# Moving the next head's product, the W3 and W4 reads and the output buffers in a fused attention, MLP and gradient kernel

## The chip, the core and the metric

The kernel runs on one core of a Trainium2 chip. The metric is the time of one execution on the device in microseconds (us), the median over repeated runs. All tensors are bfloat16 in DRAM; sums are kept in float32.

The engines of the core work side by side, each through its own list of instructions in order: PE multiplies matrices, DVE does elementwise work and reductions, ACT scales, copies and takes exponentials, POOL and SP here only issue DMAs. A DMA is issued on an engine's queue (SP's or POOL's here) and carried out by 16 DMA engines that all queues share.

## What is computed

One query token of width 640 passes through an attention over 32 heads, each with its own cache of 8192 keys and 8192 values of width 192, and then an MLP; the results are the output and the gradients of a scalar product with `grad_out` in nine inputs.

```python
# forward
mod = silu(c) @ w_mod                       # six vectors: sa, ca, ga, sb, cb, gb
h   = layernorm(x) * (1 + ca) + sa
q   = h @ wq                                # 32 heads of 192
p   = softmax(q K^T / sqrt(192))            # per head, over 8192 keys
o   = p V
x   = x + ga * (o @ wo)
h   = layernorm(x) * (1 + cb) + sb
x   = x + gb * (h + gelu(layernorm(h) @ w3) @ w4)   # the mixer part falls away in what is differentiated and shown here
...
# backward: out_0 = x; out_1.. = gradients of A_x, k_cache, v_cache, wq, wo, w3, w4, c, w_mod
```

Nearly all bytes are in the caches: K and V are 100.7 MB each, and so are their gradients dK and dV. V is read twice, once in the forward part and once in the backward part; dK and dV are outer products (a column of weights over the keys times a row of 192) and are only written.

## The kernel before

**Tiles.** A head's K or V is cut into two halves, each one tile of 128 partitions by 32 keys by 192 (1536 KB, called t = 0 and 1). Scaling and multiplying go by quarters of a head (q = 0 to 3, 16 keys per partition).

**Forward part.** The loop at L545 runs over i = 1 to 33 and has three heads in flight. For head i it makes the scores and the softmax; for head i-1 it scales K by the exponentials; for head i-2 and i-1 it multiplies V by scaled K on PE. Its pieces, by name:

- `fwd_load` (L331) reads a half of V of head i-1 and the same half of K of head i+1, both through SP. V tiles come from the pool `fv` with three buffers, K tiles from `big` with five (and every sixth from a pool of one).
- `fwd_mult(h, t)` (L344) multiplies a half of K by q on DVE, into a tile `prod` of a pool with two buffers. `fwd_ssum(h, t)` (L352) adds its 24 pieces up on PE; `fwd_red` (L361) and `fwd_comb` (L365) finish the scores, `fwd_max` (L373) spreads the maximum, and `fwd_exp` (L376) takes the negative maximum on DVE (`negm`), the exponential on ACT (`E_f`), and copies of it on DVE (`P2h`, `E_all`).
- `fwd_scale(h, q)` (L405) scales a quarter of K into a tile EK: 8 of its 16 rows on ACT (L391), the rest on DVE (L399). It needs `E_f` and `P2h`.
- `fwd_kv(h, q)` (L434) is the multiplication of V by EK, in three parts A, B and K; its last reader sets V's and EK's buffers free. `fwd_keep` and `fwd_keepB` (L453, L464) take a head's result out of PSUM.

In an iteration the order was: scale(i-1, 0 and 1), ssum(i, 0), mult(i, 1), kv(i-2, 2 and 3), scale(i-1, 2), mult(i+1, 0), keep and keepB of head i-2, ssum(i, 1), red(i), scale(i-1, 3), kv(i-1, 0), the maximum, kv(i-1, 1), exp(i).

**Between the parts.** W3 (640 by 1536) and W4 (1536 by 640) lie in tiles `w_t` of `big`. They were read by four DMAs of POOL (L557 to L562): W3 and seven of twelve row blocks of W4 in iteration 31, the last five in iteration 32. `dg_some` (L504) makes 12 dot products with W4 on DVE. From the last head's result a chain of small steps leads over two layernorms, `u` (L736, W3), the transposed W3 (L631), `dn2` (L764) and wo to `do`, and then to the first dV tile (L1079).

**Backward part.** The loop at L1083 runs over i = 0 to 31, from the last head down. Per head: `bwd_dv` (L898) makes two dV tiles, 20 of 32 rows on ACT and the rest on DVE; `bwd_mult` (L889) multiplies both halves of V by do on DVE and adds up on PE; `bwd_ds` (L911); `bwd_dk` (L918) makes two dK tiles on DVE. dV and dK tiles come from the five buffers of `big` and are written by POOL's DMAs (L909, L924). Other gradients (wo, w3, w4, wq, w_mod) are spread over the iterations as jobs J0, J1 and J2; the jobs for wq and w_mod have pools of their own (`side`), whose last use is in iteration 24.

**Order.** `pin_order` (L53) fixes the order of PE, DVE and ACT to that of the text of the kernel. The order on SP and POOL, and which free buffer a tile gets, is settled when the program is built.

Of the kernel before, what the change touches and what calls it, by code (L numbers as in the profile page):

```python
# [9 lines left out]
BF16 = mybir.dt.bfloat16  # L10
# [10 lines left out]
def kernel(  # L21
# [26 lines left out]
    nc = tc.nc  # L48
# [16 lines left out]
    P = 128  # L65
    D = A_x.shape[-1]
    _, HQ, S, DH = A_k_cache.shape
# [156 lines left out]
    def big_tile(name):  # L224
        return big.tile([P, JH, DH], BF16, name=name, tag="big")
# [105 lines left out]
    def fwd_load(h, t):  # L331
        if 0 <= h < HQ:
            st[h]["V"].append(load_v(fv, h, t))
        if h + 2 < HQ and (h + 2, t) not in K_st:
            K_st[h + 2, t] = load_k(h + 2, t)
# [37 lines left out]
    def fwd_max(h, st):  # L373
        nc.tensor.matmul(st["sm"][:, P : 2 * P], lhsT=st["m1"].to_broadcast([P, P]), rhs=ident_f, start=True, stop=True)

    def fwd_exp(h, st):  # L376
        negm = fsm.tile([P, 1], FP32, name="negm")
        nc.vector.tensor_reduce(out=negm, in_=st["sm"][:, P : 2 * P], axis=AX.X, op=ALU.max, negate=True)  # L378
        E_f = fsm.tile([P, J], FP32, name="E_f")
        nc.scalar.activation(out=E_f, in_=st["sm"][:, 0:J], func=ACT.Exp, bias=negm, scale=1.0, accum_out=rowsum[:, h : h + 1])  # L380
        P2h = fsm.tile([P, J, 2], BF16, name="P2h")
        nc.vector.tensor_copy(out=P2h, in_=E_f[:, :, None].to_broadcast([P, J, 2]))
        nc.vector.tensor_copy(out=E_all[:, h, :], in_=E_f)
        st["E_f"], st["P2h"], st["EK"] = E_f, P2h, []
# [20 lines left out]
    def fwd_scale(h, q, st):  # L405
        fwd_scale_act(h, q, st)
        fwd_scale_dve(h, q, st)
# [26 lines left out]
    def fwd_kv(h, q, st):  # L434
        fwd_kvA(h, q, st)
        fwd_kvB(h, q, st)
        fwd_kvK(h, q, st)

    def fwd_wo(h, st):
        if h % 2 == 1:  # L440
            c0 = 3 * (h // 2)
            st["wo"] = fwo.tile([P, 3, D], BF16, name="wo_t")
            nc.sync.dma_start(out=st["wo"], in_=wo_v[:, c0 : c0 + 3, :])
# [51 lines left out]
    def flat(tl):  # L495
        return tl.rearrange("p j d -> p (j d)")

    def w3n(i, lo, hi):
        return w_t[0][:, i * F + lo : i * F + hi] if i < 4 else w_t[1][:, lo:hi]

    def w4n(f, lo, hi):
        return w_t[1][:, F + f * D + lo : F + f * D + hi] if f < 7 else w_t[2][:, (f - 7) * D + lo : (f - 7) * D + hi]

    def dg_some(f0, f1):  # L504
        jk_t = fpr.tile([P, JH, DH], BF16, name="prod").rearrange("p j d -> p (j d)")
# [39 lines left out]
    for i in range(1, HQ + 2):  # L545
        if i == HQ + 1:
            nc.scalar.activation(out=warm, in_=eps_c, func=ACT.Sqrt)
        c, p, pp = 2 <= i < HQ, 0 <= i - 1 < HQ, 0 <= i - 2 < HQ
        n = i + 1 < HQ
        fwd_load(i - 1, 0)  # L550
        if p:
            fwd_scale(i - 1, 0, st[i - 1])
            fwd_scale(i - 1, 1, st[i - 1])
        fwd_load(i - 1, 1)
        if i == HQ - 1:
            w_t = [flat(big_tile(f"w_t{k}")) for k in range(2)]
            nc.gpsimd.dma_start(out=w_t[0].rearrange("p (i n) -> p i n", n=F), in_=B_w3[0 : 4 * P, :].rearrange("(i p) n -> p i n", p=P))  # L557
            nc.gpsimd.dma_start(out=w_t[1][:, 0:F], in_=B_w3[4 * P : 5 * P, :])
            nc.gpsimd.dma_start(out=w_t[1][:, F : F + 7 * D].rearrange("p (f n) -> p f n", n=D), in_=B_w4[0 : 7 * P, :].rearrange("(f p) n -> p f n", p=P))
        if i == HQ:  # L560
            w_t.append(flat(big_tile("w_t2")))
            nc.gpsimd.dma_start(out=w_t[2][:, 0 : 5 * D].rearrange("p (f n) -> p f n", n=D), in_=B_w4[7 * P : 12 * P, :].rearrange("(f p) n -> p f n", p=P))  # L562
        if p:
            fwd_wo(i - 1, st[i - 1])
        if c:
            fwd_ssum(i, 0, st[i])
            fwd_mult(i, 1, st[i])
        if i % 2 == 1 and n:
            q_pb[(i + 1) // 2] = pair_bc(fsm, q_bf, (i + 1) // 2, "q_pb", st[max(i - 1, 1)]["sm"])
        if i % 2 == 0 and i >= 4:  # L570
            fwd_ao((i - 4) // 2, st[i - 3]["wo"], st[i - 1]["sm"])
            fwd_ao_add((i - 4) // 2, st[i - 1]["sm"])
        if pp:
            fwd_kv(i - 2, 2, st[i - 2])
            fwd_kvA(i - 2, 3, st[i - 2])
            fwd_kvB(i - 2, 3, st[i - 2])
            fwd_kvK(i - 2, 3, st[i - 2])
        if i > HQ:
            dg_some(7, NFC)
        if p:  # L580
            fwd_scale(i - 1, 2, st[i - 1])
            if i % 2 == 0:
                fwd_tot(i - 1, st[i - 1]["sm"])
        if n:
            fwd_mult(i + 1, 0, st[i + 1])
        if pp:
            fwd_keep(i - 2, st[i - 2])
            fwd_keepB(i - 2, st[i - 2])
            if i % 2 == 1:
                fwd_o((i - 2) // 2)  # L590
        if p and i % 2 == 0:
            fwd_rinv(i - 1, st[i - 1]["sm"])
        if c:
            fwd_ssum(i, 1, st[i])
            fwd_red(i, st[i])
        if p:
            fwd_scale(i - 1, 3, st[i - 1])
            if i == 1:
                q_out(1, NWQ)
            fwd_kvA(i - 1, 0, st[i - 1])  # L600
            fwd_kvB(i - 1, 0, st[i - 1])
        if c:
            fwd_comb(i, st[i])
        if p:
            fwd_kvK(i - 1, 0, st[i - 1])
        if c:
            fwd_max(i, st[i])
        if p:
            fwd_kv(i - 1, 1, st[i - 1])
        if c:  # L610
            fwd_exp(i, st[i])
        if i == HQ:
            dg_some(0, 7)
    SB = [1024]
    w_t.append(flat(big_tile("w_t3")))
    NB3 = JH * DH // P
# [1 line left out]
    def w3T(blk, n=1):  # L618
        if blk < NB3:
            return w_t[3][:, blk * P : (blk + n) * P]  # L620
        c0 = 5 * D + (blk - NB3) * P
        return w_t[2][:, c0 : c0 + n * P]

    w3T_next = [0]
# [264 lines left out]
    def bwd_mult(h, t):  # L889
# [5 lines left out]
            nc.tensor.matmul(bst[h]["dP_ps"][:, t * JH : (t + 1) * JH, :], lhsT=ident_bf, rhs=V_sb[:, :, k * DS : (k + 1) * DS], start=(k == 0), stop=(k == NDS - 1))  # L895
        freed.add(("v", h, t))

    def bwd_dv(h, t, na=NAV // 2, parts=1):  # L898
        o = big_tile("dV")
        j0 = t * JH  # L900
        doh = vec_of(do_pb, h)
        for jj in range(na):
            nc.scalar.activation(out=o[:, jj, :], in_=doh, func=ACT.Copy, scale=bst[h]["PF"][:, j0 + jj : j0 + jj + 1])  # L903
        n = JH // parts
        for r0 in range(0, JH, n):
            r1 = r0 + n
            ra = max(r0, na)
            pairs_outer(o[:, ra:r1, :], bst[h]["P2h"][:, j0 + ra : j0 + r1, :], doh, r1 - ra)
            st2.dma_start(out=dV_hd[h][:, j0 + r0 : j0 + r1, :], in_=o[:, r0:r1, :])  # L909
# [6 lines left out]
        bst[h]["dS2"] = dS2  # L916

    def bwd_dk(h, t, parts=1):  # L918
        o = big_tile("dK")
        n = JH // parts  # L920
        for r0 in range(0, JH, n):
            j0 = t * JH + r0
            pairs_outer(o[:, r0 : r0 + n, :], bst[h]["dS2"][:, j0 : j0 + n, :], vec_of(q_pb, h), n)
            st2.dma_start(out=dK_hd[h][:, j0 : j0 + n, :], in_=o[:, r0 : r0 + n, :])  # L924
# [93 lines left out]
    NPH = 10  # L1018
# [64 lines left out]
    for i in range(HQ):  # L1083
        h, nxt = HS[i], HS[i + 1] if i + 1 < HQ else None
        if i % 2 == 1 and nxt is not None:
            bwd_dob(nxt // 2)
        for f in J0[i]:
            f()
        if i <= AHEAD:
            for t in range(2):  # L1090
                bwd_mult(h, t)
        ring_load()
        if i - 1 in dq:
            fin_dq(*dq.pop(i - 1))
        if i == 0:
            fin_c_copy(PS[0], 1, c_first)
        if nxt is not None:
            bwd_pf(nxt)
            for t in range(2):
                bwd_dv(nxt, t)  # L1100
        if i < NPH:
            hook(i)
        if i == 3:
            bcast_cols(du_bf, 0, NFC, du_bc, act_copy)
        for f in J1[i]:
            f()
        bwd_ds(h)
        if i >= AHEAD and nxt is not None:
            for t in range(2):
                bwd_mult(nxt, t)  # L1110
        bwd_dk(h, 0)
        bwd_dk(h, 1, 1 if nxt is not None else 4)
        if i in cps:
            fin_c_copy(*cps.pop(i))
        if i == 1:
            mid_cols()
            job_mid()
            dve_copy(dmod_bf[:, 2 * NDC : 6 * NDC], dmod_c[:, 2 * NDC : 6 * NDC])
        if i == NPH - 1:
            fin_dq(*dq.pop(i))  # L1120
            for cm in reversed(mm_cms):
                cm.__exit__(None, None, None)
            for nm, b in (("in", 1), ("out", 4), ("bc", 1)):
                side[nm] = ctx.enter_context(tc.tile_pool(name="side" + nm, bufs=b, side="right", reuse_waits="tile"))
        for f in J2[i]:
            f()
    pin_order(first_ins)


# [28 lines left out]
```

## Time and profile before

| | |
|---|---|
| time, median of 3 runs | 1394.95 us (1394.62 to 1397.5) |
| the profiled execution's own time | 1396.62 us |
| its span, first to last instruction | 1394.8 us |
| DMA | 570.81 MB, 409 GB/s over the span |
| of it through SP's queue | 339.16 MB |
| of it through POOL's queue | 229.85 MB |
| DVE busy | 1078.9 us (77%) |
| ACT busy | 964.2 us (69%) |
| PE busy | 856.1 us (61%) |

A row of the stretches view gives, for a stretch of the span, each engine's busy time with its count of instructions, the clock that PE was granted as a share of full speed, the share of time that the 16 DMA engines were busy, and the bytes that they moved per second. A row of the timeline gives start, length, engine, line, operation and tiles, and in brackets how long the engine stood idle just before and what ended that. The forward part runs to about 560 us, the steps between the parts to about 581 us, the backward part to the end. Iteration 24 of the backward loop ends at 1246 us.

### The profile page before, as it was taken

The page shows a single profiled execution, that of the slowest core. Times are in us where ns is not written, and L with a number is a line of the kernel's source. Part 1 is how long each engine was busy: PE and PEld are TensorE (multiplying, and loading weights), DVE is VectorE, ACT ScalarE, POOL GpSimd, SP SyncE. Part 2 cuts the span into 40 slices and gives each one's busy share as a digit, 9 for nine tenths or more (in the row PEclk, how much of TensorE's full clock was granted, in tenths as well). Part 3 has the DMA queues.
Part 4 walks back from the last instruction along what each step waited for, and adds up shares of the span by engine and source line. Part 5 has one row for each costly group of instructions (what it writes and reads, how often), then busy time and mean ns, then how long its engine had stood idle before and what let it go on. Part 6 is the DMA issues. An engine that isn't in the chain of part 4 may idle for free. (4 is left out here: it accounts for less than half of the span.)

```text
span 1394.8 us, 28118 instructions
## 1 busy us (share of the span) xinstructions
PE 856.1 (61%) x11519; PEld 672.9 (48%) x11519; DVE 1078.9 (77%) x1276; ACT 964.2 (69%) x2633; POOL 114.9 (8%) x207
## 2 busy tenths in 40 slices
PE   3699999999999999737635642443432435323342
PEld 3577777777777777626525541322222223212231
DVE  3588878878888886699988984975768659666796
ACT  1487778877777787786795586566766766566582
POOL 0000000000000000011101110211111111111011
PEclk9799999999999999666656665666675666755666
DMA  9999999999999999699999999999999999999988
GB/s 392 418 420 417 415 410 416 418 404 402 418 412 408 413 417 403 241 384 397 426 427 425 425 428 427 427 427 427 427 427 424 424 424 419 426 409 416 407 352 367
DMA packets 71711, 570.81 MB, mean 409 GB/s; under 512 B 6878, under 2 KB 18398, under 8 KB 31134
## 3 DMA queue, kind: packets, MB, share of 16 engines
q1 hardware_dynamic: 46496, 339.16, 59.2%
q0 software_dynamic: 25056, 229.85, 39.1%
q8 instruction: 90, 1.47, 0.4%
q14 instruction: 39, 0.32, 0.1%
q10 hardware_dynamic: 30, 0.00, 0.0%
HBM read 343.08 MB, written 225.91 MB: 408 GB/s over the span
## 5 line engine op out<-in xcount | busy, mean ns | idle before, releaser
L903 ACT ACTIVATE dV<-do_pb,PF 128x192 bf16<-128x192 bf16 x1260 | 439.3, 440 | 90.9 <-DMA out_dram<-dK 60.6
L895 PE MATMUL dP_ps<-V_sb,ident_bf 128*128 128x256 bf16 x1536 | 232.1, 326 | 258.6 <-DVE V_sb L131 258.6
L391 ACT ACTIVATE EK<-K_sb,E_f 128x192 bf16<-128x192 bf16 x1024 | 364.5, 442 | 22.1 <-PE kb_ps L432 14.0
L895 PEld LDWEIGHTS <-ident_bf 128*128 128x128 bf16 x1536 | 179.4, 117 | 311.0 <-issue 177.9
L880 DVE TENSOR_TENSOR dK<-dS,q_pb 128x6144 bf16<-128x6144 bf16 (+1 forms) x67 | 213.2, 3211 | 47.0 <-DMA out_dram<-dK 43.2
L131 DVE TENSOR_TENSOR prod<-K_sb,q_pb 128x6144 bf16<-128x6144 bf16 x64 | 214.6, 3354 | 23.5 <-DMA K_sb<-in_A_k_cache_dram 18.0
L131 DVE TENSOR_TENSOR V_sb<-V_sb,do_pb 128x6144 bf16<-128x6144 bf16 x64 | 211.8, 3350 | 6.6 <-DMA V_sb<-in_A_v_cache_dram 6.6
L416 PE MATMUL ps_a<-EK,V_sb 128*128 128x193 bf16 x2048 | 202.1, 252 | 3.1 <-DMA V_sb<-in_A_v_cache_dram 2.3
L416 PEld LDWEIGHTS <-V_sb 128*128 128x128 bf16 x2048 | 175.6, 100 | 21.8 <-issue 17.4
L880 DVE TENSOR_TENSOR dV<-P2h,do_pb 128x2304 bf16<-128x2304 bf16 (+1 forms) x65 | 87.2, 1368 | 56.1 <-DMA out_dram<-dV 44.0
L399 DVE TENSOR_TENSOR EK<-K_sb,P2h 128x1536 bf16<-128x1536 bf16 x128 | 121.6, 950 | 0.0
L424 PE MATMUL ps_b<-EK,V_sb 128*64 128x193 bf16 x2048 | 110.8, 250 | 8.2 <-DVE MB_all L134 7.9
L359 PE MATMUL S_ps<-prod,ident_bf 64*64 64x256 bf16 x3072 | 99.7, 277 | 7.2 <-DVE prod L131 7.2
L424 PEld LDWEIGHTS <-V_sb 128*64 128x64 bf16 x2048 | 84.4, 109 | 28.9 <-issue 28.7
L359 PEld LDWEIGHTS <-ident_bf 64*64 64x64 bf16 x3072 | 82.3, 109 | 22.8 <-issue 22.3
L380 ACT ACTIVATE E_f<-sm_ps,negm 128x64 f32<-128x64 f32 x32 | 10.1, 315 | 104.9 <-DVE negm L378 104.9
L909 POOL DMA_DIRECT2D out_dram<-dV x65 | 34.8, 535 | 462.6 <-ACT dV L903 313.7
L432 PE MATMUL kb_ps<-EK,hot_bf 128*32 128x384 bf16 x1024 | 65.9, 335 | 2.0 <-DVE q_bf L304 2.0
L981 PEld LDWEIGHTS <-ident_bf 128*128 128x128 bf16 x112 | 14.5, 130 | 91.4 <-issue 88.9
L194 ACT CAST do_pb<-bc_ps 128x384 bf16<-128x384 f32 x16 | 7.5, 470 | 69.0 <-PE bc_ps L190 69.0
L939 ACT ACTIVATE wq_o<-wq_bc,ha_f 128x1536 bf16<-128x1536 bf16 x12 | 18.5, 1565 | 47.8 <-DMA out_dram<-wq_o 47.8
L924 POOL DMA_DIRECT2D out_dram<-dK x67 | 37.1, 554 | 165.0 <-DVE dK L880 126.5
(249 smaller groups left out, 821.8 us busy)
## 6 DMA issues: line engine op xcount, KB each, us to landing
V_sb<-in_A_v_cache_dram SPq DMA_DIRECT2D x126, 1536.0 KB, 11.8
K_sb<-in_A_k_cache_dram SPq DMA_DIRECT2D x64, 1536.0 KB, 13.7
out_dram<-dV POOLq DMA_DIRECT2D x63, 1536.0 KB, 18.5
out_dram<-dK POOLq DMA_DIRECT2D x63, 1536.0 KB, 20.8
wq<-in_A_wq_dram SPq DMA_DIRECT2D x3, 2560.0 KB, 33.9
wo_t<-in_A_wo_dram SPq DMA_DIRECT2D x16, 480.0 KB, 12.4
out_dram<-dwo POOLq DMA_DIRECT2D x16, 480.0 KB, 19.5
wq<-in_A_wq_dram SPq DMA_DIRECT2D x4, 1920.0 KB, 29.7
```

Source lines behind the costliest of these rows:

```text
L131: nc.vector.tensor_tensor(out=out, in0=a, in1=b, op=ALU.mult)
L359: nc.tensor.matmul(st["S_ps"][c0 : c0 + 64, r, t * JH : (t + 1) * JH, :], lhsT=ident_bf[64 * r : 64 * r + 64, 64 * r : 64 * r + 64], rhs=p ...
L391: nc.scalar.activation(out=EK[:, jj, 0:DH], in_=K_st[h, t][:, r * JQ + jj, :], func=ACT.Copy, scale=st["E_f"][:, j : j + 1])
L399: nc.vector.tensor_tensor(out=EK[:, NA:JQ, 0:DH].rearrange("p j (d r) -> p j d r", r=2), in0=K_st[h, t][:, r * JQ + NA : (r + 1) * JQ, :]. ...
L416: nc.tensor.matmul(st["A_ps"][:, 0 : DH + 1], lhsT=V_sb[:, r * JQ + jj, a0:a1], rhs=EK[:, jj, 0 : DH + 1], start=(q == 0 and jj == 0), sto ...
L424: nc.tensor.matmul(st["B_ps"][g : g + 64, 0 : DH + 1], lhsT=V_sb[:, r * JQ + jj, b0:b1], rhs=EK[:, jj, 0 : DH + 1], start=(q == 0 and jj < ...
L432: nc.tensor.matmul(kb_ps[g : g + 32, 0 : 2 * DH], lhsT=hot_bf[:, HQ - 1 - h : 2 * HQ - 1 - h], rhs=EK[:, jj : jj + 2, 0:DH], start=(h == 0 ...
L880: nc.vector.tensor_tensor(out=o.rearrange("p j (d r) -> p j d r", r=2), in0=pairs[:, :, None, :].to_broadcast([P, n, NP2, 2]), in1=vec.rea ...
L895: nc.tensor.matmul(bst[h]["dP_ps"][:, t * JH : (t + 1) * JH, :], lhsT=ident_bf, rhs=V_sb[:, :, k * DS : (k + 1) * DS], start=(k == 0), sto ...
L903: nc.scalar.activation(out=o[:, jj, :], in_=doh, func=ACT.Copy, scale=bst[h]["PF"][:, j0 + jj : j0 + jj + 1])
L909: st2.dma_start(out=dV_hd[h][:, j0 + r0 : j0 + r1, :], in_=o[:, r0:r1, :])
L924: st2.dma_start(out=dK_hd[h][:, j0 : j0 + n, :], in_=o[:, r0 : r0 + n, :])
```

## The change

Four things are moved or added.

- `fwd_mult(i+1, 0)` is no longer done behind scale(i-1, 2), but inside `fwd_exp(i)`: on DVE between `negm` and `P2h`.
- `fwd_kv(i-2, 2)` stands ahead of `fwd_ssum(i, 0)` on PE instead of behind it.
- W3 and W4 are read by SP instead of POOL, cut otherwise: nine row blocks of W4 into the first tile in iteration 31 (ahead of the second half of V of head 30), then in iteration 32, behind V of the last head, three blocks of W4 and two of W3 into the second tile and three of W3 into the third. `dg_some` is cut 9 and 3 instead of 7 and 5.
- Behind the jobs of iteration 24 the `side` pools are closed and a pool `more` with three tiles is opened. From iteration 25 the tiles for dV and dK come from eight buffers: of each eight tiles the first, fourth and sixth from `more`, the others from `big`.

```diff
-    def fwd_exp(h, st):
+    def fwd_exp(h, st, between=lambda: None):
         negm = fsm.tile([P, 1], FP32, name="negm")
         nc.vector.tensor_reduce(out=negm, in_=st["sm"][:, P : 2 * P], axis=AX.X, op=ALU.max, negate=True)
         E_f = fsm.tile([P, J], FP32, name="E_f")
         nc.scalar.activation(out=E_f, in_=st["sm"][:, 0:J], func=ACT.Exp, bias=negm, scale=1.0, accum_out=rowsum[:, h : h + 1])
+        between()
         P2h = fsm.tile([P, J, 2], BF16, name="P2h")
...
+    w_t = []
+    W4_N, W3_N = 9, 2
+    W4_R = NFC - W4_N
+
     def w3n(i, lo, hi):
-        return w_t[0][:, i * F + lo : i * F + hi] if i < 4 else w_t[1][:, lo:hi]
+        c0 = W4_R * D + i * F if i < W3_N else (i - W3_N) * F
+        return w_t[1 if i < W3_N else 2][:, c0 + lo : c0 + hi]
 
     def w4n(f, lo, hi):
-        return w_t[1][:, F + f * D + lo : F + f * D + hi] if f < 7 else w_t[2][:, (f - 7) * D + lo : (f - 7) * D + hi]
+        c0 = f % W4_N * D
+        return w_t[f // W4_N][:, c0 + lo : c0 + hi]
+
+    def load_wt(k):
+        w_t.append(flat(big_tile(f"w_t{k}")))
+        if k < 2:
+            f0, f1 = (0, W4_N) if k == 0 else (W4_N, NFC)
+            nc.sync.dma_start(out=w_t[k][:, 0 : (f1 - f0) * D].rearrange("p (f n) -> p f n", n=D), in_=B_w4[f0 * P : f1 * P, :].rearrange("(f p) n -> p f n", p=P))
+        if k > 0:
+            i0, i1, c0 = (0, W3_N, W4_R * D) if k == 1 else (W3_N, NDC, 0)
+            nc.sync.dma_start(out=w_t[k][:, c0 : c0 + (i1 - i0) * F].rearrange("p (i n) -> p i n", n=F), in_=B_w3[i0 * P : i1 * P, :].rearrange("(i p) n -> p i n", p=P))
...
+        if i == HQ - 1:
+            load_wt(0)
         fwd_load(i - 1, 1)
-        if i == HQ - 1:
-            w_t = [flat(big_tile(f"w_t{k}")) for k in range(2)]
-            nc.gpsimd.dma_start(out=w_t[0].rearrange("p (i n) -> p i n", n=F), in_=B_w3[0 : 4 * P, :].rearrange("(i p) n -> p i n", p=P))
-            nc.gpsimd.dma_start(out=w_t[1][:, 0:F], in_=B_w3[4 * P : 5 * P, :])
-            nc.gpsimd.dma_start(out=w_t[1][:, F : F + 7 * D].rearrange("p (f n) -> p f n", n=D), in_=B_w4[0 : 7 * P, :].rearrange("(f p) n -> p f n", p=P))
-        if i == HQ:
-            w_t.append(flat(big_tile("w_t2")))
-            nc.gpsimd.dma_start(out=w_t[2][:, 0 : 5 * D].rearrange("p (f n) -> p f n", n=D), in_=B_w4[7 * P : 12 * P, :].rearrange("(f p) n -> p f n", p=P))
         if p:
             fwd_wo(i - 1, st[i - 1])
+        if i == HQ:
+            load_wt(1)
+            load_wt(2)
+        if pp:
+            fwd_kv(i - 2, 2, st[i - 2])
         if c:
             fwd_ssum(i, 0, st[i])
             fwd_mult(i, 1, st[i])
...
         if pp:
-            fwd_kv(i - 2, 2, st[i - 2])
             fwd_kvA(i - 2, 3, st[i - 2])
...
         if i > HQ:
-            dg_some(7, NFC)
+            dg_some(9, NFC)
...
-        if n:
-            fwd_mult(i + 1, 0, st[i + 1])
...
+        first = lambda: fwd_mult(i + 1, 0, st[i + 1]) if n else None
         if c:
-            fwd_exp(i, st[i])
+            fwd_exp(i, st[i], first)
+        else:
+            first()
         if i == HQ:
-            dg_some(0, 7)
+            dg_some(0, 9)
...
+    more, out_n = [None], [0]
+
+    def out_tile(name):
+        if more[0] is None:
+            return big_tile(name)
+        out_n[0] += 1
+        if out_n[0] % 8 in (1, 4, 6):
+            return more[0].tile([P, JH, DH], BF16, name=name, tag="more")
+        return big_tile(name)
+
     def bwd_dv(h, t, na=NAV // 2, parts=1):
-        o = big_tile("dV")
+        o = out_tile("dV")
...
     def bwd_dk(h, t, parts=1):
-        o = big_tile("dK")
+        o = out_tile("dK")
...
-            for nm, b in (("in", 1), ("out", 4), ("bc", 1)):
-                side[nm] = ctx.enter_context(tc.tile_pool(name="side" + nm, bufs=b, side="right", reuse_waits="tile"))
+            side_cms = [tc.tile_pool(name="side" + nm, bufs=b, side="right", reuse_waits="tile") for nm, b in (("in", 1), ("out", 4), ("bc", 1))]
+            for nm, cm in zip(("in", "out", "bc"), side_cms):
+                side[nm] = cm.__enter__()
         for f in J2[i]:
             f()
+        if i == NPH + 14:
+            for cm in reversed(side_cms):
+                cm.__exit__(None, None, None)
+            more[0] = ctx.enter_context(tc.tile_pool(name="more", bufs=3, side="right", reuse_waits="tile"))
```

More of the change, by code (lines that the diff above doesn't have):

```diff
@@ L620, in w3T @@
             return w_t[3][:, blk * P : (blk + n) * P]
-        c0 = 5 * D + (blk - NB3) * P
+        c0 = (NDC - W3_N) * F + (blk - NB3) * P
         return w_t[2][:, c0 : c0 + n * P]
```

## The prediction

> **What bounds the kernel now.** I read the 40 slices of the page first, then the stretches.
>
> ```profile
> DMA  9999999999999999699999999999999999999988
> ...
> core 0: us, PE busy (x) PEld busy (x) DVE busy (x) ACT busy (x) POOL busy (x), PEclk, DMA share, GB/s
> 70.00:520.00 450.00, 422.21 (x7686) 335.90 (x7687) 373.66 (x550) 352.10 (x1033) 0.00 (x0) 0.98 1.00 413
> 520.00:560.00 40.00, 37.95 (x639) 30.55 (x632) 29.27 (x66) 31.05 (x90) 3.27 (x4) 1.00 1.01 405
> 560.00:600.00 40.00, 29.71 (x403) 24.21 (x403) 27.37 (x82) 32.60 (x84) 2.17 (x4) 0.65 0.63 232
> 600.00:1246.00 646.00, 283.40 (x1743) 216.17 (x1742) 506.48 (x455) 438.28 (x1121) 91.30 (x159) 0.65 1.01 424
> 1246.00:1327.00 81.00, 24.01 (x158) 18.09 (x158) 53.99 (x36) 50.90 (x147) 7.99 (x15) 0.64 0.99 410
> 1327.00:1360.00 33.00, 15.41 (x102) 11.81 (x102) 32.83 (x18) 27.17 (x80) 4.13 (x8) 0.69 0.82 345
> ...
> 1360.00:1390.00 30.00, 7.69 (x48) 5.77 (x48) 23.92 (x15) 9.65 (x28) 4.97 (x10) 0.63 1.00 411
> ```
>
> DMA is the bound: its share is about 1.00 nearly everywhere. The change moves no byte less, so it can only win time in which the DMA engines stand idle. There are three such places: short ones inside the forward part, 560 to 600, and 1327 to 1360, where DVE is busy 32.83 of 33 us and stores come too slowly. I price each by its shortfall in GB/s.
>
> The forward part's holes are in four of its heads:
>
> ```profile
> 190.00:200.00 10.00, 9.98 (x160) 7.60 (x161) 7.08 (x14) 6.14 (x19) 0.00 (x0) 0.83 0.97 388
> ...
> 290.00:300.00 10.00, 10.00 (x217) 7.87 (x213) 8.79 (x8) 8.56 (x27) 0.00 (x0) 1.00 0.93 364
> 320.00:330.00 10.00, 10.00 (x160) 8.18 (x160) 7.08 (x12) 7.29 (x22) 0.00 (x0) 0.84 0.93 364
> 410.00:420.00 10.00, 7.16 (x142) 5.52 (x140) 8.22 (x19) 5.40 (x17) 0.00 (x0) 1.00 0.98 399
> ```
>
> Against 413 GB/s they lose (25 + 49 + 49 + 14) / 413 x 10 = 3.3 us. The timeline ahead of the first shows why:
>
> ```profile
> 184.24 3.36 DVE L131 TENSOR_TENSOR prod<-K_sb,q_pb 128x6144 bf16<-128x6144 bf16 x1 [1.70 <-DMA K_sb<-in_A_k_cache_dram]
> ...
> 188.04 0.86 PE L424 MATMUL ps_b<-EK,V_sb 128*64 128x193 bf16 x16 [0.99 <-DVE MB_all L134]
> ...
> 190.02 0.44 PE L368 MATMUL sm_ps<-S,stack_f 128*64 128x64 f32 x4 [1.11 <-DVE S L363]
> ...
> 192.31 0.31 ACT L380 ACTIVATE E_f<-sm_ps,negm 128x64 f32<-128x64 f32 x1 [4.49 <-DVE negm L378]
> ```
>
> DVE stands 1.70 us at mult(i+1, 0) for a K tile that is late. keepB and red are queued behind it, so PE waits 0.99 and 1.11 us, then runs at a mean clock of 0.83 in the next 10 us, frees V late, and the DMA queue runs dry.
>
> **The change, part by part.**
>
> *The product behind the maximum.* The same 3.36 us on DVE, 6 to 7 us later in the head. A late K tile no longer holds keepB and red; by the new place it has landed, since the waits are short:
>
> ```profile
> DVE prod L131 <- DMA K_sb<-in_A_k_cache_dram: 13.7, 13, 1.8
> ```
>
> What stands behind it now is `P2h`, the DVE scaling of quarters 0 and 1, mult(i+1, 1), and PE's ssum(i+1, 1), which waits for that. An undisturbed head shows whether this fits:
>
> ```profile
> 393.39 1.50 PE L359 MATMUL S_ps<-prod,ident_bf 64*64 64x256 bf16 x48
> ...
> 398.16 0.29 DVE L378 TENSOR_REDUCE negm<-sm_ps 128x1 f32<-128x128 f32 x1 [0.62 <-PE sm_ps L374]
> ...
> 398.92 0.23 DVE L382 CAST P2h<-E_f 128x128 bf16<-128x128 f32 x1 [0.47 <-ACT E_f L380]
> ...
> 400.85 0.95 DVE L399 TENSOR_TENSOR EK<-K_sb,P2h 128x1536 bf16<-128x1536 bf16 x1
> ...
> 401.72 3.35 DVE L131 TENSOR_TENSOR prod<-K_sb,q_pb 128x6144 bf16<-128x6144 bf16 x1
> ...
> 407.63 1.50 PE L359 MATMUL S_ps<-prod,ident_bf 64*64 64x256 bf16 x48
> ```
>
> `negm` ends at 398.45. Then the moved product 3.4, `P2h` and `E_all` 0.3, two scalings of 1.0 each and mult(i+1, 1) 3.35 make 407.5, and PE comes to its sums at 407.63: a fit with 0.1 us to spare. So PE's head stays 407.63 - 393.39 = 14.2 us, while the DMA needs 4 x 1536 KB plus half a wo tile, 6.5 MB at 413 GB/s, 15.8 us: 1.6 us of cover per head. If that cover is gone, the sums are late, then V's buffers. kv(i-2, 2) ahead of ssum(i, 0) gives PE 2.9 us of work while the moved product ends (401.9 here) and frees an EK buffer sooner; the same instructions, nothing added.
>
> Bounds: 0 (the starved heads come back for another cause) to -3.3 us (all four go). I take **-2.5**, three quarters, because the wait shown is the only one ahead of each hole and it is what the move takes out of the way. A price on the other side is the rival below.
>
> The Trainium skill, "TensorE: Matmul & The Clock Gate", section "What's actually happening", says the clock halves after an idle window of about 3.4 us. The two waits here are 2.1 us together and the clock was 0.83 behind them, so smaller gaps suffice in this kernel; by the page these heads would not have slowed, and the term would be only the waits' own 2.1 us per hole, which the DMA's cover would hide.
>
> *W3 and W4 by SP, in line.* The same bytes (3.9 MB), three tiles, four DMAs instead of four, issued by SP instead of POOL. Around 560 us PE, not DMA, leads:
>
> ```profile
> 525.73 0.29 DVE L378 TENSOR_REDUCE negm<-sm_ps 128x1 f32<-128x128 f32 x1 [0.58 <-PE sm_ps L374]
> ...
> 535.03 1.50 PE L359 MATMUL S_ps<-prod,ident_bf 64*64 64x256 bf16 x48
> ...
> 539.75 0.89 POOL L562 DMA_DIRECT2D w_t<-in_B_w_dram  x1 [5.83 <-ACT EK L391]
> ...
> 549.32 1.52 PE L416 MATMUL ps_a<-EK,V_sb 128*128 128x193 bf16 x16 [0.78 <-ACT MA_all L459]
> ...
> 554.38 1.54 PE L416 MATMUL ps_a<-EK,V_sb 128*128 128x193 bf16 x16 [0.49 <-DMA V_sb<-in_A_v_cache_dram]
> ...
> 580.68 3.43 DVE L880 TENSOR_TENSOR dV<-P2h,do_pb 128x3072 bf16<-128x3072 bf16 x2 [1.11 <-ACT do_pb L194]
> ```
>
> PE waits for the last V only 0.49 us at 554.38. If W no longer shares the engines with it, that is the most to win. The hole of 560 to 600 (a shortfall of 17 us) lies behind the chain to the first dV at 580.68, which has no step less. Queue order: SP waits for the W tiles' buffers (POOL found its last one free at 539.75), behind which V of head 31 would stand; PE needs its first half only at 549.32, so some 5 us of wait are covered. Against it stands the new order in the last heads, which have no DMA to hide under: `negm` of head 30 ends at 526.0, and 3.4 + 0.3 + 2.3 + 3.35 make 535.4 for mult(31, 1), where PE is ready at 535.03; with red and the DVE steps behind it, 0.3 to 0.8 us. Sum: -0.5 to +0.8; I take **+0.3**.
>
> *Eight tiles.* No instruction is added; waits on buffers go.
>
> ```profile
> DVE dV L880 <- DMA out_dram<-dK: 7.8, 2, 3.9
> DVE dV L880 <- DMA out_dram<-dV: 6.6, 2, 5.9
> DVE dK L880 <- DMA out_dram<-dK: 5.7, 2, 3.2
> ...
> 1327.03 1.36 DVE L880 TENSOR_TENSOR dV<-P2h,do_pb 128x2304 bf16<-128x2304 bf16 x1 [5.02 <-DMA out_dram<-dV]
> ...
> 1377.20 6.83 DVE L880 TENSOR_TENSOR dK<-dS,q_pb 128x6144 bf16<-128x6144 bf16 x5
> ```
>
> The first three rows are DVE's waits between 1246 and 1327: 20.1 us, the 5.02 among them. From 1327 DVE works without a pause to 1384, and the DMA starves. Three tiles more let it run ahead by three stores, 3 x 1.57 MB / 411 GB/s = 11.5 us of DMA time, more than the hole: (411 - 345) / 411 x 33 = 5.3 us by rate, 5.9 us by share (0.18 x 33). DVE then ends near 1384 - 11.5 = 1372, and the end is the DMA's. The first tile from `more` has to wait for the old users of its place:
>
> ```profile
> L995 POOL DMA_DIRECT2D out_dram<-wm_o x6: 540/542/582, 1187.8 to 1244.9; - x6
> ...
> DMA to landing us min/median/max: 17.5/22.9/24.0
> ...
> 1248.87 13.92 ACT L903 ACTIVATE dV<-do_pb,PF 128x192 bf16<-128x192 bf16 x40
> ...
> 1266.25 3.36 DVE L880 TENSOR_TENSOR dK<-dS,q_pb 128x6144 bf16<-128x6144 bf16 x1 [2.47 <-DMA out_dram<-dK]
> ```
>
> The last wm_o store is issued at 1244.9 and lands by about 1268. If only the second `more` tile lies on those (the first on the wq and w_mod input tile, read for the last time in iteration 23), it is dK of iteration 25, which started at 1266.25 anyway: nothing lost. If the first lies there, dV of head 26 waits from 1249 to 1268, DVE stands 19 us, the two dK stores issued before it carry the DMA for 7.5 us, and some 3 to 6 us are given back. Bounds -6.7 (5.9 and 0.8 for a small hole near 1287) to 0; I take **-6.0**, since the pool's first tile takes the place of the pool closed last in order of opening, `in`.
>
> [...]
>
> **Sum.** Against the profiled execution's own 1396.62 us (span 1394.8): -2.5 + 0.3 - 6.0 = -8.2, so 1388.4. The median of the runs lies 1.7 below that execution: **1386.8 us**.
>
> **The rivals.**
>
> *Only the end wins* (1395.0 - 6.0 + 0.3 = 1389.3). The forward holes come from DMA jitter and return elsewhere. For it: the clock was 1.00 in 290 to 300 and 410 to 420. Against: a late K tile precedes each.
>
> *Only the forward part wins* (1395.0 - 2.5 + 0.3 = 1392.8). The `more` tiles wait for the wm_o stores, or the reads of V just end sooner and the stretch of stores alone, in which DVE is too slow, begins sooner. Against: DVE's 20 us of waits are longer than the hole.
>
> *Slower: PE starves on the moved product* (about 1407). The place is ssum(i, 1). The fit has 0.1 us to spare, the cover is 1.6 us. From a delay of over 1.6 us per head on (a late EK buffer or K tile behind `negm`, with half a clock after it), every head costs DMA time; at 1.2 us, what 290 to 300 lost (49 / 413 x 10), in half of 30 heads that is 18 us, so 1395.0 - 6.0 + 0.3 + 18. For it: no slack on DVE between `negm` and the sums. Against: DVE is busy 373.66 of 450 us, and its wait for EK buffers falls into the moved product's time.
>
> *Nothing happens* (1395): bytes bind and the holes move.
>
> **How the numbers follow.** Forecast 0.60, only the end 0.17, only the forward part 0.07, nothing 0.04, slower 0.12. Runs of this kernel differ by about 0.2%, 2.8 us. Faster by more than that (below 1392.2): 0.60 + 0.17 + a little of the third, 0.78; within it 0.10; slower 0.12. The forecast's own bounds are -10.5 to -3, 1384 to 1392; with the third case and a little below, 1383.5 to 1394, which leaves out the slower case and few others.
>
> **What would show it.** Forward: no wait of DVE for K at L131 above 1 us, ACT's wait for `negm` below the 4.49 us, no stretch of 10 us under 400 GB/s between 70 and 520. Between: the first dV within 1 us of 580.7, less what the forward part won. End: DVE's waits for dV and dK stores from 1246 on under 10 us, 1327 to 1360 at over 400 GB/s, DVE's last dK near 1365 to 1375. Wrong would be PE waits at L359 above 1 us per head, or a DMA share under 0.95 between 1250 and 1290.

## The result, and the profile after

| | before | after |
|---|---|---|
| time, median of 4 runs each | 1395.76 us (1394.62 to 1397.5) | 1387.58 us (1386.67 to 1389.87) |
| ratio after to before, 95% interval | | 0.9943 (0.9926 to 0.996) |
| span of the profiled execution | 1394.8 us | 1388.1 us |
| that execution's own time | 1396.62 us | 1389.87 us |

The time fell by 8.2 us, and 1386.8 us was forecast. The terms of the forecast's sum do not hold, though: one was three times too small, one was nearly nothing, and a third did far more than its price says. The stretches view of the changed kernel, in the stretches used for the kernel before (start and end, each engine's busy time and count, granted PE clock, DMA share, GB/s):

```profile
70.00:520.00 450.00, 419.20 (x7772) 334.87 (x7771) 369.78 (x555) 359.78 (x1049) 0.00 (x0) 1.00 1.01 418
520.00:560.00 40.00, 36.17 (x581) 28.03 (x575) 28.49 (x76) 28.71 (x79) 0.00 (x0) 0.96 0.96 368
560.00:600.00 40.00, 26.32 (x340) 22.38 (x340) 29.57 (x65) 33.23 (x87) 3.35 (x6) 0.59 0.70 269
600.00:1246.00 646.00, 283.51 (x1748) 216.69 (x1747) 502.42 (x460) 435.86 (x1113) 89.91 (x157) 0.65 1.01 423
1246.00:1327.00 81.00, 29.63 (x204) 23.00 (x204) 68.14 (x39) 59.66 (x172) 9.85 (x20) 0.66 1.00 414
1327.00:1360.00 33.00, 15.40 (x96) 11.49 (x96) 32.89 (x17) 26.92 (x78) 4.24 (x8) 0.69 1.01 427
1360.00:1390.00 30.00, 0.00 (x0) 0.00 (x0) 8.18 (x8) 0.00 (x0) 3.24 (x6) 0.54 0.65 269
```

Three things stand out. The forward part runs at 418 GB/s instead of 413. The hole at 1327 to 1360 is filled, 427 instead of 345. And two new holes are there: 520 to 560 (368 instead of 405) and the last 30 us, where the share falls to 0.65.

**Forward.** The four stretches that had starved, and the stretch ahead of them, in the changed kernel:

```profile
190.00:200.00 10.00, 10.00 (x218) 7.95 (x214) 7.30 (x11) 7.31 (x21) 0.00 (x0) 1.00 1.02 427
290.00:300.00 10.00, 10.00 (x176) 8.11 (x174) 8.34 (x16) 6.95 (x21) 0.00 (x0) 1.00 1.02 419
320.00:330.00 10.00, 9.64 (x170) 7.54 (x168) 8.49 (x12) 6.56 (x21) 0.00 (x0) 1.00 1.02 417
410.00:420.00 10.00, 9.28 (x197) 7.62 (x198) 7.11 (x14) 8.38 (x25) 0.00 (x0) 1.00 1.00 412
...
20.00:70.00 50.00, 33.42 (x629) 27.96 (x630) 30.76 (x32) 18.55 (x53) 0.00 (x0) 1.00 1.02 421
```

and that last stretch in the kernel before:

```profile
20.00:70.00 50.00, 29.05 (x587) 24.67 (x588) 27.99 (x30) 18.57 (x52) 0.00 (x0) 0.80 1.02 421
```

All four holes are gone. Ahead of 70 us the PE clock was 0.80 and is 1.00; in product_only and w_pool, two kernels below that share the moved product, it is 0.83. What each engine waits for between 100 and 500 us (us in total, times, longest), before and then after:

```profile
ACT E_f L380 <- DVE negm L378: 71.0, 25, 4.9
...
DVE prod L131 <- DMA K_sb<-in_A_k_cache_dram: 13.7, 13, 1.8
```

```profile
ACT E_f L380 <- DVE negm L378: 52.0, 25, 2.6
...
DVE prod L131 <- DMA K_sb<-in_A_k_cache_dram: 32.8, 24, 2.1
PE ps_a L417 <- DMA V_sb<-in_A_v_cache_dram: 22.5, 20, 1.7
...
PE S_ps L359 <- DVE prod L131: 1.3, 1, 1.3
```

ACT waits less for `negm`; DVE waits more for K than before, not less; and PE, which led before, now waits for V. The timeline at one head shows where the K waits have gone:

```profile
184.52 0.29 DVE L378 TENSOR_REDUCE negm<-sm_ps 128x1 f32<-128x128 f32 x1 [0.58 <-PE sm_ps L374]
184.73 3.35 DVE L131 TENSOR_TENSOR prod<-K_sb,q_pb 128x6144 bf16<-128x6144 bf16 x1
...
191.83 3.36 DVE L131 TENSOR_TENSOR prod<-K_sb,q_pb 128x6144 bf16<-128x6144 bf16 x1 [1.63 <-DMA K_sb<-in_A_k_cache_dram]
```

The moved product follows `negm` with no wait; of its 25 in this window none waits for K. The waits all stand at mult(i, 1), the second half, 7 us later, where PE still has work: PE's own waits for `prod` come to 1.3 us.

**End.** DVE's waits for stores from 1246 on, and its last dK:

```profile
DVE dV L895 <- DMA out_dram<-dV: 8.9, 2, 5.9
...
DVE dV L895 <- DMA out_dram<-wm_o: 2.9, 1, 2.9
...
DVE dK L895 <- DMA out_dram<-dK: 0.8, 1, 0.8
```

```profile
1361.42 6.83 DVE L895 TENSOR_TENSOR dK<-dS,q_pb 128x6144 bf16<-128x6144 bf16 x5
```

Waits for dV and dK stores fell from 25.1 us (11.6, 7.8 and 5.7 in the kernel before) to 9.7, and DVE ends at 1368 instead of 1384. The wait for `wm_o` is that of the first tile from `more`: it did lie on the old stores, but cost 2.9 us and not the 19 that the prediction feared for this case. The program ends only 6.7 us earlier all the same.

### The profile page after: what moved, and what is told of

Its sections match the earlier page's. It is cut to its first block, busy times and chain, and to the rows that moved or that the text cites. A ratio compares the mean times of both kernels' runs of the same rounds, so it can differ in the third digit from the quotient of the medians.

```text
span 1388.1 us, 28075 instructions
## 1 busy us (share of the span) xinstructions
PE 850.3 (61%) x11519; PEld 670.2 (48%) x11519; DVE 1073.6 (77%) x1276; ACT 966.5 (70%) x2633; POOL 111.7 (8%) x203
## 5 line engine op out<-in xcount | busy, mean ns | idle before, releaser
L417 PE MATMUL ps_a<-EK,V_sb 128*128 128x193 bf16 x2048 | 197.1, 248 | 28.2 <-DMA V_sb<-in_A_v_cache_dram 25.8
L417 PEld LDWEIGHTS <-V_sb 128*128 128x128 bf16 x2048 | 171.5, 98 | 48.3 <-DMA V_sb<-in_A_v_cache_dram 41.4
L895 DVE TENSOR_TENSOR dV<-P2h,do_pb 128x2304 bf16<-128x2304 bf16 (+1 forms) x65 | 86.9, 1368 | 40.7 <-DMA out_dram<-dV 35.7
L359 PE MATMUL S_ps<-prod,ident_bf 64*64 64x256 bf16 x3072 | 101.3, 280 | 9.0 <-DVE prod L131 8.4
L359 PEld LDWEIGHTS <-ident_bf 64*64 64x64 bf16 x3072 | 84.7, 110 | 24.5 <-issue 23.6
```

The lines of the kernel that those rows point to most:

```text
L359: nc.tensor.matmul(st["S_ps"][c0 : c0 + 64, r, t * JH : (t + 1) * JH, :], lhsT=ident_bf[64 * r : 64 * r + 64, 64 * r : 64 * r + 64], rhs=p ...
L417: nc.tensor.matmul(st["A_ps"][:, 0 : DH + 1], lhsT=V_sb[:, r * JQ + jj, a0:a1], rhs=EK[:, jj, 0 : DH + 1], start=(q == 0 and jj == 0), sto ...
L895: nc.vector.tensor_tensor(out=o.rearrange("p j (d r) -> p j d r", r=2), in0=pairs[:, :, None, :].to_broadcast([P, n, NP2, 2]), in1=vec.rea ...
```

## The experiments

All are compared with the kernel before on the same chip; a ratio's interval is 95%. One table carries the places in their profiles that the readings use, in us from the start of the span. "Full until" is when all 16 DMA engines were last busy at once, and "last packet" the end of the last data transfer, both from the packet records, the first good to about half a microsecond.

| kernel | median us | ratio (interval) | `negm` of head 30 | last store issued | full until | last packet |
|---|---|---|---|---|---|---|
| before | | | 525.73 | 1384.33 | 1391.0 | 1392.1 |
| after | 1387.58 | 0.9943 (0.9926 to 0.996) | 518.26 | 1368.72 | 1377.6 | 1386.1 |
| product_only | 1398.82 | 1.002 (1.0009 to 1.0031) | 518.40 | 1388.36 | 1394.2 | 1395.8 |
| w_only | 1394.8 | 0.9996 (0.9985 to 1.0008) | 525.34 | 1381.19 | 1387.4 | 1388.7 |
| tiles_only | 1394.69 | 0.9997 (0.9986 to 1.0008) | 525.95 | 1372.73 | 1380.4 | 1390.7 |
| no_mult | 1393.0 | 0.9983 (0.9972 to 0.9995) | 525.15 | 1373.62 | 1380.7 | 1391.0 |
| no_kv | 1387.49 | 0.9943 (0.9926 to 0.996) | 518.16 | 1366.62 | 1374.3 | 1384.1 |
| no_w | 1398.89 | 1.0022 (1.0012 to 1.0032) | 518.14 | 1377.19 | 1384.5 | 1395.2 |
| w_pool | 1395.76 | 0.9998 (0.9987 to 1.0009) | 518.13 | 1374.40 | 1382.0 | 1392.3 |
| no_tiles | 1388.33 | 0.9951 (0.9933 to 0.9968) | 518.31 | 1376.40 | 1382.6 | 1383.9 |
| sp_store | 1388.61 | 0.9947 (0.9932 to 0.9962) | 518.24 | 1378.97 | 1383.6 | 1385.9 |
| sp_five | 1390.58 | 0.9964 (0.995 to 0.9979) | 518.38 | 1380.98 | 1385.6 | 1386.2 |
| q_swap | 1392.14 | 0.9977 (0.9963 to 0.9992) | 518.45 | 1373.02 | 1382.5 | 1390.9 |

### Each part alone

product_only is the kernel before with the moved product and the moved kv:

```diff
         if c:
-            fwd_exp(i, st[i])
+            fwd_exp(i, st[i], first)       # first = fwd_mult(i + 1, 0), between negm and P2h
```

> The kernel before with the moved product and kv(i-2, 2) alone. By the prediction's terms: 2.2 us faster (bounds 0 to 3.3, less 0.3 in the last heads). By the profile after, where negm of head 30 stands at 518.26 instead of 525.73: some 5 to 7 us faster, with the landing of K near 20 us instead of 13.7, and DVE waiting for K behind the maximum. If both are wrong and the forward part was fast by chance: within 1 us of before.

w_only is the kernel before with W3 and W4 read by SP as in the change:

```diff
+        if i == HQ - 1:
+            load_wt(0)
         fwd_load(i - 1, 1)
...
+        if i == HQ:
+            load_wt(1)
+            load_wt(2)
```

> The kernel before with W3 and W4 read by SP, alone. By the prediction: within 0.5 us of before. By the hole of the profile after between 520 and 535 (368 GB/s in 520:560 against 405): 1 to 3 us slower, with a wait of PE for V ahead of the last head's products, since nothing fills the DMA queue while SP stands at a V buffer.

tiles_only is the kernel before with the pool `more`:

```diff
-        o = big_tile("dV")
+        o = out_tile("dV")
...
+            more[0] = ctx.enter_context(tc.tile_pool(name="more", bufs=3, side="right", reuse_waits="tile"))
```

> The kernel before with eight tiles from iteration 25 alone. By the prediction: 6 us faster (0 to 6.7), 1327 to 1360 filled. By the end of the profile after, where the DMA engines fall from 16 to 1 busy between 1377 and 1386: 1 to 3 us faster, the hole moved behind the last store as one late DMA engine.

None of the three is faster. W by SP and eight tiles are within their intervals of no change, and the moved product alone is slower by 0.2%, which none of its three expectations allowed. Yet `negm` of head 30 comes 7.3 us earlier with it (518.40 against 525.73). So the forward part gives all of its gain, and something behind it takes more back. The timeline of product_only shows the place:

```profile
536.80 2.77 PE L417 MATMUL ps_a<-EK,V_sb 128*128 128x193 bf16 x16 [6.05 <-DMA V_sb<-in_A_v_cache_dram]
...
542.10 0.29 DVE L378 TENSOR_REDUCE negm<-sm_ps 128x1 f32<-128x128 f32 x1 [0.62 <-PE sm_ps L374]
542.43 0.32 ACT L380 ACTIVATE E_f<-sm_ps,negm 128x64 f32<-128x64 f32 x1 [11.42 <-DVE negm L378]
```

PE stands 6.05 us for a V tile, works on at half clock (16 multiplications in 2.77 us instead of 1.54), and `negm` of the last head comes 23.7 us behind that of head 30, where the kernel before takes 14.2. At that time POOL reads W. How long a V tile takes from issue to landing among those issued between 505 and 540 us (count, KB each, median us) in before, product_only and after:

```profile
V_sb<-in_A_v_cache_dram SPq DMA_DIRECT2D x4, 1536.0 KB, 11.8
```

```profile
V_sb<-in_A_v_cache_dram SPq DMA_DIRECT2D x3, 1536.0 KB, 23.3
```

```profile
V_sb<-in_A_v_cache_dram SPq DMA_DIRECT2D x4, 1536.0 KB, 16.2
```

### The change without one part

no_mult puts the product back behind scale(i-1, 2), no_kv puts kv(i-2, 2) back behind ssum(i, 0), no_w reads W by POOL as before, no_tiles keeps five tiles. Each is the change with those lines of its diff left out; the two moves are

```diff
-            fwd_exp(i, st[i], first)
+            fwd_exp(i, st[i])
...
+        if n:
+            fwd_mult(i + 1, 0, st[i + 1])      # no_mult: behind fwd_scale(i - 1, 2)
```

```diff
-        if pp:
-            fwd_kv(i - 2, 2, st[i - 2])
         if c:
             fwd_ssum(i, 0, st[i])
...
+            fwd_kv(i - 2, 2, st[i - 2])        # no_kv: behind fwd_ssum(i, 0)
```

> The changed kernel with mult(i+1, 0) back behind scale(i-1, 2), so that DVE stands at a late K tile ahead of keepB and red again. By the prediction's reason: the starved heads come back (10 us stretches under 400 GB/s, a halved clock behind them), negm of head 30 near 524 to 526, 5 to 8 us slower than the changed kernel. If the move of kv(i-2, 2) made the gain: within 2 us of the changed kernel.

> The changed kernel with kv(i-2, 2) back behind ssum(i, 0). If the moved product alone makes the forward part faster: negm of head 30 near 518 and the time within 1 us of the changed kernel. If PE then stands waiting for the late product: negm of head 30 at 522 or later, PE waits at the sums of over 0.5 us per head, 3 us or more slower.

Without the moved product the forward gain is gone (525.15) and 5.4 us of time with it. Without the moved kv nothing changes, in the time or in the forward part.

```diff
-            load_wt(0)                          # no_w: L557 to L562 of the kernel before in its place
+            nc.gpsimd.dma_start(out=w_t[0]..., in_=B_w3[0 : 4 * P, :]...)
```

> The changed kernel with W3 and W4 read by POOL as before. By the prediction: the same as the changed kernel to 0.5 us, 8 us under before. If SP's order costs the hole between 520 and 535: 1 to 3 us faster than the changed kernel, 9 to 11 us under before.

```diff
-        o = out_tile("dV")
+        o = big_tile("dV")                      # no_tiles, and the same for dK
```

> The changed kernel with five tiles for dV and dK to the end. By the prediction: 6 us slower than the changed kernel. By the alone run of the tiles (0.6 us by medians, the last DMA engine late by 10 us): 0.5 to 2 us slower, with the DMA engines ending together within 2 us.

Without W by SP the change is slower than the kernel before, where both expectations had it 8 us faster or more: the part that is worth nothing by itself is worth 11 us here. Without the tiles it loses 0.75 us, less than the runs can tell.

### Which of W's three differences counts

w_pool has the change's cut of W and its places in the text, and only another issuing engine:

```diff
-            nc.sync.dma_start(out=w_t[k]...
+            nc.gpsimd.dma_start(out=w_t[k]...
```

> The changed kernel with the same four reads of W3 and W4, cut and placed as in the change, issued on POOL's queue instead of SP's. If it is the queue that matters (on POOL's, W takes half of the engines from the V tiles that PE by then waits for, a wait of 6.05 us in the profile with the product alone): 8 to 12 us slower than the changed kernel, with a PE wait for V of over 4 us around 530. If it is the cut or the moment: within 2 us of the changed kernel. By the prediction, which gave the queue no price: the same as the changed kernel.

It loses 8.2 of the 11 us (7.7 by the ratios), so it is mostly the queue. PE's waits for V between 500 and 560 us in w_pool, and in the change:

```profile
PE ps_a L417 <- DMA V_sb<-in_A_v_cache_dram: 7.3, 3, 5.8
```

```profile
PE ps_a L417 <- DMA V_sb<-in_A_v_cache_dram: 3.3, 3, 1.6
```

V tiles issued between 505 and 540 us land after 23.2 us (median) in w_pool and after 16.2 in the change. Two queues with work share the 16 engines. As long as V tiles are early, it does not matter that W's 3.9 MB are moved beside them (moving W to SP alone, w_only, gains nothing); once the moved product has brought PE up to the DMA, V tiles are waited for and W's share is taken out of PE's time. In SP's queue three of the four reads of W stand behind the last V tile instead. The Trainium skill, "DMA: Bandwidth & Descriptors", section "Issuing engines are not separate DMA queues", says that issuing from several engines saves only the small time of the issue itself. Here the issuing engine alone is worth 8 us (w_pool against the change), since it decides what goes first.

SP's order has its price too. In the change SP waits for V's buffers with W queued behind, and the DMA engines go partly idle. Two stretches of the changed kernel:

```profile
520.00:525.00 5.00, 4.87 (x106) 3.59 (x100) 4.29 (x8) 5.00 (x16) 0.00 (x0) 1.00 0.88 335
525.00:530.00 5.00, 4.35 (x96) 3.41 (x88) 4.87 (x9) 4.95 (x16) 0.00 (x0) 1.00 0.78 275
```

In the same 10 us the kernel before moved 408 and 404 GB/s. The timeline of the changed kernel adds:

```profile
536.95 0.62 SPq L515 DMA_DIRECT2D w_t<-in_B_w_dram  x1
...
575.65 3.43 DVE L895 TENSOR_TENSOR dV<-P2h,do_pb 128x3072 bf16<-128x3072 bf16 x2 [1.11 <-ACT do_pb L194]
```

W's second tile is issued at 536.95 only, and of the 7.5 us won at `negm` of head 30 there are 5.0 left at the first dV (575.65 against 580.68). From the one to the other the change takes 2.4 us more than the kernel before; in the profiles of the five other kernels with the moved product and W by SP it is 1.3 to 3.8.

### What binds the end

tiles_only fills the hole and issues its last store 11.6 us earlier, as the prediction says it should, and the time stays. Its last rows:

```profile
1327.00:1360.00 33.00, 14.08 (x88) 10.65 (x89) 31.59 (x19) 28.86 (x84) 3.74 (x7) 0.69 1.01 429
...
1375.00:1380.00 5.00, 0.00 (x0) 0.00 (x0) 0.00 (x0) 0.00 (x0) 0.00 (x0) 0.50 0.98 402
1380.00:1385.00 5.00, 0.00 (x0) 0.00 (x0) 0.00 (x0) 0.00 (x0) 0.00 (x0) 0.50 0.30 127
1385.00:1390.00 5.00, 0.00 (x0) 0.00 (x0) 0.00 (x0) 0.00 (x0) 0.00 (x0) 0.50 0.06 27
```

A share of 0.06 is 1/16, and 27 GB/s a sixteenth of the 429 above: one DMA engine is alone at work. The packet records show its packets end to start, 12288 bytes in 0.46 us or 6144 in 0.23, with no pause. The kernel before has its engines together to the end:

```profile
1385.00:1390.00 5.00, 0.00 (x0) 0.00 (x0) 0.00 (x0) 0.00 (x0) 0.00 (x0) 0.50 0.99 392
```

In the table every kernel with eight tiles and its stores on one queue has 8.4 to 10.7 us from "full until" to the last packet, and those with five have 0.6 to 1.6. In the kernels with the long end most engines stop within 2 us of "full until", a few later, and the last one is alone for 3.0 to 6.1 us.

A late engine is in the kernel before as well. In the worst of its hole the row is

```profile
1354.00:1356.00 2.00, 2.00 (x20) 1.78 (x18) 2.00 (x2) 1.97 (x7) 0.25 (x1) 0.99 0.08 31
```

31 GB/s, little more than one engine's rate: fifteen had run out of stores and one had not, until 1356.5. In all of 1327 to 1360 the packet records leave only 0.4 us in which none of the 16 is busy. If it is the same engine that is late each time, the hole that the prediction priced by the rate of all 16 cost it no more than that; that it is the same one is not shown, since the records don't number the engines.

Two more kernels ask what makes an engine late. sp_store is the change with the last heads' stores issued by SP, and sp_five the same with five tiles; POOL's queue is then empty at the end:

```diff
+        if i == HQ - 4:
+            tail_q[0] = nc.sync                 # dV and dK stores from here on; before, nc.gpsimd
```

> The change, with the dV stores of the last three heads and the dK stores of the last four issued by SP, which has nothing left to load by then, instead of POOL. Leading theory (one of the 16 DMA engines is some 8 to 10 us behind the others by its own work, whoever issues, and eight tiles only let the other fifteen run ahead of it): the median stays within 2 us of the change's 1387.6, all 16 engines are last busy together at 1374 to 1378, and the last packet still ends 8 to 10 us later. Rival (the lag is made by POOL's queue): the last packet follows within 3 us, and the time falls to 1379 to 1382. Third (each store by SP takes longer to start, or two queues in turn cost rate): slower than 1390, with a rate under 420 GB/s between 1310 and 1375.

> The change with five tiles for dV and dK, and with the same last stores by SP. Leading theory: within 2 us of the 1388.3 that five tiles gave with POOL's stores, the gap between all engines busy and the last packet 1 to 2 us as there, since five stores in flight bound how far the engines can come apart. If SP's issue itself is quicker or slower than POOL's: the landings of the last dV stores differ by over 1 us from those by POOL and the time by 2 us or more.

The time of sp_store stays, as the leading theory said, but the engines end together (1383.6 and 1385.9), as it did not. Its rows say why this decides nothing:

```profile
1310.00:1340.00 30.00, 8.07 (x54) 6.22 (x54) 17.29 (x11) 15.51 (x45) 0.00 (x0) 0.61 1.01 429
1340.00:1365.00 25.00, 12.34 (x68) 8.91 (x69) 24.89 (x14) 19.66 (x57) 0.00 (x0) 0.64 0.87 363
1365.00:1375.00 10.00, 4.24 (x30) 3.15 (x28) 9.93 (x6) 0.00 (x0) 0.00 (x0) 0.84 0.83 349
```

With two queues at work DVE is idle for 12.7 of 30 us, its waits there being for old stores, and from 1340 on it is DVE that is short again, as in the kernel before: a late engine can catch up in that hole. sp_five lies 2.3 us above no_tiles by the medians and 1.8 by the ratios, at the edge of what its expectation set as a difference; the cause stays open.

q_swap therefore changes the queues over for the whole backward part, so that no store goes through POOL and DVE keeps its lead:

```diff
-    st2 = nc.gpsimd
+    st2 = nc.sync
+    ldq[0] = nc.gpsimd                          # the reads of V, wo, wq, w_mod
```

> The change, with the queues of the backward part changed over: every store there (dV, dK and the other gradients) is issued by SP, and the reads of V, wo, wq and w_mod by POOL. Theory A (one DMA engine falls behind in the part with reads and writes, whichever queue the stores use): all 16 engines are last busy together some 8 to 10 us before the last packet, the row of the last 5 us shows about 27 GB/s, one engine's rate, and the time stays within 2 us of the change's 1387.6. Theory B (the engine falls behind because the stores go through POOL's queue): the gap is under 3 us with DVE's last dK before 1372, and the time falls to 1379 to 1383. Against both: slower than 1391, if reads by POOL come late, which would show as waits of DVE for V of over 10 us from 600 on.

```profile
600.00:1246.00 646.00, 281.64 (x1748) 216.49 (x1747) 501.50 (x459) 434.96 (x1113) 36.68 (x61) 0.66 1.01 418
...
1375.00:1380.00 5.00, 0.00 (x0) 0.00 (x0) 0.00 (x0) 0.00 (x0) 0.00 (x0) 0.50 1.00 422
1380.00:1385.00 5.00, 0.00 (x0) 0.00 (x0) 0.00 (x0) 0.00 (x0) 0.00 (x0) 0.50 0.67 270
1385.00:1388.00 3.00, 0.00 (x0) 0.00 (x0) 0.00 (x0) 0.00 (x0) 0.00 (x0) 0.50 0.13 52
1388.00:1392.00 4.00, 0.00 (x0) 0.00 (x0) 0.00 (x0) 0.00 (x0) 0.00 (x0) 0.50 0.05 18
```

DVE's last dK starts at 1365 here, and the gap is 8.4 us again, with every store by SP. So stores through POOL's queue are not needed for it. The kernel as a whole is 4.6 us slower than the change, outside what either theory gave: 600 to 1246 runs at 418 GB/s instead of 423, and the wait of DVE for V that the third case named is not there. Why the rate is lower stays open. Which engine is late, and where it falls behind, stays open. The Trainium skill, "DMA: Bandwidth & Descriptors", section "Latency and other measured facts", says that DMA engines 7 and 15 are usually slower than the others, and offers as a guess that the descriptors of POOL's DMAs crowd their ports. The records here don't number the engines, and a late one is there also without stores by POOL, so the guess is neither confirmed nor excluded for the reads.

## Why the prediction was right in its total, and where its steps were not

**The product behind the maximum: mechanism right, size wrong.** Taken at -2.5 with a bound of -3.3; it is -7.3 to -7.6 at `negm` of head 30 in every kernel that has it, and at most 0.6 in those that do not. The bound counted only four stretches far under 413 GB/s, in a window that began at 70 us. Two sources lay outside it. First, `negm` comes earlier before the DMA has gained anything: by 2.0 us at head 2 (77.70 against 79.73) and by 6.2 at head 5 (122.08 against 128.28), while by 180 us the packets have moved the same bytes to 0.1 MB. The clock ahead of 70 us does not explain it: product_only and w_pool, with 0.83 there, win 2.2 us at head 2 as well. What does stays open. Second, more stretches than the four were short: by 520 us the change has moved 2.2 MB more, which is 5.4 us at 413 GB/s, and the four holes account for 3.3 of it. The kernel before also has 403 GB/s at 330 to 340, 378 at 420 to 430 and 399 at 450 to 460. A share of 1.00 over a long stretch did not mean that nothing could be won. K tiles now land 20.0 us after their issue in the median instead of 13.7, which fits more reads standing in the queue.

**"No wait of DVE for K above 1 us": wrong.** DVE waits 32.8 us for K between 100 and 500 us, up to 2.1 at a time, and PE 22.5 us for V: the DMA has become the slower side. DVE's waits do little harm where they stand now, which is the point of the move. The rival in which PE starves on the moved product did not come: PE's waits at L359 are 1.3 us. The 0.1 us of slack was enough, since the DMA, not DVE, paces the heads.

**W by SP: this step failed.** It was taken by itself, from the 0.49 us that PE waited for V in the kernel before, "the most to win". That row belongs to a kernel in which PE led. With the moved product PE is at the DMA's heels when W comes, and the order of W against V is worth 8 us by the queue and 11 with its cut and place. It is a condition for the first part to show at all: the forecast would have been wrong by its whole amount without it. What was seen rightly is only that something is lost in its turn: 2.4 us between `negm` of head 30 and the first dV, not 0.3.

**Eight tiles: this step failed as well.** -6.0 was taken; alone they give 0.6 and within the change 0.75 us, both inside the intervals. Each sign that the prediction named came true: waits of 9.7 us, 427 GB/s between 1327 and 1360, the last dK at 1361 to 1368. What failed is the sentence "the end is the DMA's", with the 16 engines taken as one. The hole of 345 GB/s was idle time of engines that were ahead, while at least one went on working in all but 0.4 us; filling it lets the first finish at 1377.6 and leaves the last at 1386.1. The rival "only the forward part wins", given 7 in 100, comes nearest to what happened, with more than three times its gain and with W by SP as its condition.

**The sum.** In the profiled execution: -7.5 forward, +2.4 between, -1.7 from the first dV to the end, together -6.7 of span with the rounding; by the medians -8.2. Counted in bytes, the lead is 2.2 MB at 520 us and 2.2 MB again at 620, 5.3 to 5.4 us at 413 GB/s, so most of the +2.4 seems to undo an earliness of `negm` that the DMA never had. Predicted were -2.5, +0.3 and -6.0. The total agrees because the errors cancel: that is luck, and no evidence for the steps. The prediction's own upper bound of -3 is not the sum of its terms' upper bounds either (0, +0.8 and 0).

## What to carry to other kernels

Before pricing two edits apart, ask what the first does to the rows that price the second: a wait of 0.5 us for a transfer was worth 8 us once another edit had used up the lead that covered it. When a DMA-bound program ends, look at the last rows in sixteenths; a share of 0.06 is one engine that finishes alone, and here more buffers only let the others wait for it longer. Bytes that compete with a tile someone waits for were better off behind it in the same queue than beside it in another.

## What was not expected of the hardware

- The last of the 16 DMA engines finished 8.4 to 10.7 us after all 16 were last busy together, at the end alone at 27 GB/s and without a pause, in all kernels with eight tiles and their stores on one queue, whichever of the two. With five tiles the end doesn't show it, only a hole does.
- From 70 to 520 us a DMA share of 1.00 went with 413 GB/s in one kernel and 1.01 with 418 in the other, on the same kinds of transfer.
- A single wait of 6.05 us for a V tile cost PE its clock: the 16 multiplications behind it took 2.77 us instead of 1.54. From 20 to 70 us the mean granted clock was 0.80 in the kernel before, 1.00 in the changed one and 0.83 in product_only, which came to head 2 as early as the changed one.
